# Snake activation: cosine on ScalarE and one VectorE pass from PSUM in place of sine, square and a product matmul; first-layer tiles of one bank

## Chip, cores, metric

One core of a Trainium2 chip. The metric is the device time of one execution in microseconds (us). PE is TensorE (matmuls), PEld its weight loads, ACT ScalarE, DVE VectorE, POOL GpSimd, SP SyncE. A ratio is the mean time of one kernel's fast runs over the mean of the other's fast runs of the same rounds, so it is not quite the ratio of the medians quoted beside it. Profiled spans (875.6 before) come from one execution each.

## The reference

```python
X = np.fft.rfft(x, axis=1)                 # x: 8 x 3008 x 256
y = np.fft.irfft(X * (filt_r + 1j*filt_i), n=3008, axis=1)
h = y.reshape(24064, 256) @ w_in           # 256 -> 2048
s = np.sin(alpha * h)
g = h + s * s / (alpha + 1e-09)
out = g @ w_out                            # 2048 -> 256
```

With a = alpha, `g @ w_out` is `(a*h + sin(a*h)**2) @ (w_out/a)`. The linear part can be folded into one 256 x 256 matrix, `h @ w_out = y @ (w_in @ w_out)`, which is what the kernel before does. Or, with `sin(u)**2 = (1 - cos(2u))/2`, the bracket is `-0.5 * ((cos(2ah) - 1) - 2ah)`.

## The kernel before

The Fourier transform is three matmul stages per batch, here called first (`pa`), middle (`pb`, products `p`, `pc`) and last (`pd`). They are threaded as small pieces into 48 "chunks" of 512 columns (four of them 384) of the two-layer network. A chunk has eight steps. A step makes two of the sixteen first-layer tiles of its chunk and one eighth of the previous chunk's projection. The spectral tiles rotate through two PSUM banks (`fps`), the hidden tiles through two tiles of two banks (`hps`), the projection through two (`ops`): together eight banks. A bank is here 512 fp32 columns of PSUM, the memory that PE writes its results to; to evacuate it is to copy it out so that PE can write there again.

```python
    fps = pool("fps", 2, PSUM)
    hps = pool("hps", 2, PSUM)
    ops = pool("ops", 2, PSUM)
    # ... cut ...
    def evac(dst, src, on_act=None):
        flip[0] ^= 1
        if flip[0] if on_act is None else on_act:
            marks["act"] = nc.scalar.copy(out=dst, in_=src)
        else:
            marks["dve"] = nc.vector.tensor_copy(out=dst, in_=src)
    # ... cut ...
    def hidden(k, jp):
        # ...
        ps = hps.tile([128, 2, 512], FP32, name=f"ph_{k}_{jp}", tag="h")
        for i in range(2):
            jb = 2 * jp + i
            for cb in range(2):
                marks["hidden"] = nc.tensor.matmul(
                                 out=ps[:, i, 0:n], lhsT=w1[:, cb, jb * 128:jb * 128 + 128],
                                 rhs=y_cols[:, cb, c0:c0 + n], start=(cb == 0), stop=(cb == 1))
        vs = v[k][:, 2 * jp:2 * jp + 2, 0:n]
        nc.scalar.activation(out=vs, in_=ps[:, :, 0:n], func=AFT.Sin)
        marks["square"] = nc.vector.tensor_tensor(out=vs, in0=vs, in1=vs, op=ALU.mult)

    def project(k, u):
        # ...
        for jb in (range(9) if half == 0 else range(9, 16)):
            nc.tensor.matmul(out=dst, lhsT=v[k][:, jb, 128 * t:128 * t + 128],
                             rhs=w2[:, jb, :], start=(jb == 0), stop=False)
        if half == 1:
            for cb in range(2):
                nc.tensor.matmul(out=dst, lhsT=y_cols[:, cb, c0 + 128 * t:c0 + 128 * t + 128],
                                 rhs=m_t[:, cb, :], start=False, stop=(cb == 1))
```

`m_t` is w_in @ w_out, prepared during chunk 0 with 32 transposes and 32 matmuls.

## Time and profile before

| | before |
|---|---|
| median time | 880.1 us (878.55 to 881.52, 4 runs) |
| PE, ACT, DVE busy | 839.0, 519.5, 505.2 us of a span of 875.6 |
| chunk 1 begins, chunk 2 begins | 72.5, 91.4 us |
| chunk 2 to chunk 47 | 756.9 us |
| from chunk 47 to the end | 27.3 us |

The page gives, for each engine, the busy time, its share of the span and the number of instructions:

```profile
span 875.6 us, 15579 instructions
PE 839.0 (96%) x6233; PEld 584.6 (67%) x6233; DVE 505.2 (58%) x890; ACT 519.5 (59%) x667; POOL 28.1 (3%) x55
```

The windows view shows two stretches from the middle of the run: length, then the busy time of each engine with its count, the granted clock, the DMA share and GB/s:

```profile
core 0: us, PE busy (x) PEld busy (x) DVE busy (x) ACT busy (x) POOL busy (x), PEclk, DMA share, GB/s
200.00:400.00 200.00, 199.05 (x1505) 140.36 (x1504) 119.11 (x209) 125.52 (x162) 4.11 (x8) 1.00 0.47 108
400.00:600.00 200.00, 199.76 (x1514) 141.07 (x1513) 120.82 (x211) 125.33 (x162) 4.11 (x8) 1.00 0.47 110
```

PE is busy to within half a per cent, but that alone proves little, because the matmuls' modelled durations overlap (0.379 us each, started 0.216 us apart). The starts say more. A matmul follows the one before after 0.216 us if that had 512 columns, 0.109 if 256, 0.041 if 94 (medians). "TensorE: Matmul & The Clock Gate" (section "Wait — 56ns, not 53.3ns?") gives N / 2.4 GHz + 2.5 ns for a warm array, and these medians agree to a nanosecond. What the starts lie apart beyond that is below called *excess*. From chunk 2 to chunk 47 it is 8.3 us of 756.9. So in the middle of the run PE really streams, and every column taken away should shorten the run.

One step of the middle stage in the timeline (start, length, engine, line, operation; in brackets the idle time before it and what ended it). This and the later timelines show chosen lines, most of the weight loads (PEld) among those left out:

```profile
310.04 0.38 PE L394 MATMUL po_2_3514<-m_t,y 128*128 128x256 f16 x2
...
310.26 1.03 PE L375 MATMUL ph_6_3556<-y,w_465 128*128 128x512 f16 x4
...
311.12 0.38 PE L179 MATMUL pb_2_3563<-t_3_0_3278,d_t 128*128 128x256 f16 x2
...
311.32 1.02 ACT L379 ACTIVATE v_3413<-ph_6_3556 128x1024 f16<-128x1024 f32 x1 [0.51 <-PE ph_6_3556 L375]
311.34 0.27 PE L198 MATMUL pc_1_3572<-p_1_0_3536,e_t 128*128 128x256 f16 x1
...
311.78 1.15 PE L390 MATMUL po_2_3514<-w_466,v_3210 128*128 128x256 f16 x9
311.98 0.69 DVE L136 CAST g_0_3540<-pc_1_3572 128x512 f16<-128x512 f32 x1 [0.74 <-PE pc_1_3572 L198]
...
312.59 0.68 DVE L380 TENSOR_TENSOR v_3413<-v_3413 128x1024 f16<-128x1024 f16 x1
...
312.76 0.59 PE L375 MATMUL ph_7_3587<-y,w_465 128*128 128x512 f16 x2
```

The first line is the product that the change removes. The step lasts 2.50 us (310.26 to 312.76): 4 x 0.216 + 15 x 0.109 = 2.50. DVE evacuates g as soon as its matmuls are done. The hidden tile needs DVE for nothing until it is squared, and its PSUM banks are free once ACT has read them.

At the start DVE stands in front of the w_out load:

```profile
64.46 1.14 DVE L338 TENSOR_SCALAR w_466<-w_out_502,rec_t 128x256 f16<-128x256 f32 x4 [2.96 <-DMA w_out_502<-in_moe_w_out_dram]
```

### The profile page before, as it was taken

Reading aid. Unit: us, or ns where it says so; the run is one execution under the profiler, and the core shown is the slowest. Engines: PE = TensorE matmul, PEld = TensorE weight load, DVE = VectorE, ACT = ScalarE, POOL = GpSimd, SP = SyncE. Lnnn points to the kernel's source line nnn. Section 1 sums busy time; section 2 is a strip of 40 time slices with the busy share of each in tenths; the row PEclk is TensorE's granted clock in tenths of the full one; section 3 lists DMA queues with packets and bytes.
Section 4 is the critical chain, followed back from the end, with each engine's and each line's share of the span. In section 5 each row is a group of like instructions: output and inputs, shape, how many; then the busy total and the mean of one; then the engine's idle time right before and its main releaser. Section 6 shows DMA issues by size and latency. Waiting matters only on the chain.

```text
span 875.6 us, 15579 instructions
## 1 busy us (share of the span) xinstructions
PE 839.0 (96%) x6233; PEld 584.6 (67%) x6233; DVE 505.2 (58%) x890; ACT 519.5 (59%) x667; POOL 28.1 (3%) x55
## 2 busy tenths in 40 slices
PE   6759999999999999999999999999999999999996
PEld 2336676667776676767776677666767677676675
DVE  4748574566646575565746566565755657444442
ACT  4545665566656665566656666566655666555551
POOL 3210000000000000000000000000000000000000
PEclk9969999999999999999999999999999999999998
DMA  9985724275344724265342653347342343411111
GB/s 218 245 233 109 176 72 122 52 160 127 72 124 95 163 77 114 61 139 141 82 108 61 155 129 80 109 96 162 82 119 60 94 105 80 116 47 37 37 37 43
DMA packets 93489, 94.96 MB, mean 108 GB/s; under 512 B 8084, under 2 KB 82852, under 8 KB 93416
## 3 DMA queue, kind: packets, MB, share of 16 engines
q1 hardware_dynamic: 84784, 75.02, 32.5%
q0 software_dynamic: 6704, 18.09, 12.6%
q10 hardware_dynamic: 1928, 0.86, 0.5%
q8 instruction: 49, 0.80, 0.4%
q14 instruction: 24, 0.20, 0.1%
HBM read 58.02 MB, written 49.81 MB: 123 GB/s over the span
## 4 chain that ended last, share of the span: by engine, by line
PE 89%; DMA 6%; DVE 2%; issue 1%; ACT 1%; SPq 0%; ACTq 0%; DVEq 0%; POOLq 0%
DMA w_out_502<-in_moe_w_out_dram 1%; DMA t_1_0_1563<-d_1_505 1%; DMA d_0_107<-t_0_3_159 1%; DMA x_0_109<-in_x_dram 1%; DMA d_2_507<-g_9_2627 1%; DMA t_0_1_176<-d_0_107 0%; DMA t_2_0_2801<-d_2_507 0%; DMA t_4_0_5257<-d_4_511 0%; DMA t_3_0_4019<-d_3_509 0%; DMA t_0_0_476<-d_0_108 0%; PE po_0_7950 L390 0%; PE po_0_5494 L390 0%; PE po_0_3038 L390 0%; PE po_0_720 L390 0%; PE po_2_4348 L390 0%
## 5 line engine op out<-in xcount | busy, mean ns | idle before, releaser
L375 PEld LDWEIGHTS <-w_465 128*128 128x128 f16 x1536 | 150.3, 98 | 100.5 <-issue 2.1
L198 PEld LDWEIGHTS <-e_t 128*128 128x128 f16 x384 | 37.8, 99 | 13.0 <-issue 2.5
L394 PEld LDWEIGHTS <-y 128*128 128x128 f16 x376 | 36.7, 98 | 4.7
L179 PEld LDWEIGHTS <-d_t 128*128 128x128 f16 x192 | 18.7, 100 | 24.4 <-issue 5.4
L156 PEld LDWEIGHTS <-wf_t 94*96 94x96 f16 x128 | 16.5, 129 | 21.8 <-issue 9.3
L380 DVE TENSOR_TENSOR v_9644<-v_9644 128x1024 f16<-128x1024 f16 x8 | 5.5, 692 | 8.0 <-ACT v_9644 L379 8.0
L380 DVE TENSOR_TENSOR v_9789<-v_9789 128x1024 f16<-128x1024 f16 x8 | 5.5, 692 | 8.0 <-ACT v_9789 L379 8.0
L380 DVE TENSOR_TENSOR v_1608<-v_1608 128x1024 f16<-128x1024 f16 x8 | 5.5, 692 | 7.7 <-ACT v_1608 L379 7.7
L380 DVE TENSOR_TENSOR v_9488<-v_9488 128x1024 f16<-128x1024 f16 x8 | 5.5, 692 | 7.7 <-ACT v_9488 L379 7.7
L380 DVE TENSOR_TENSOR v_943<-v_943 128x1024 f16<-128x1024 f16 x8 | 5.5, 691 | 7.7 <-ACT v_943 L379 7.7
L380 DVE TENSOR_TENSOR v_3898<-v_3898 128x1024 f16<-128x1024 f16 x8 | 5.5, 690 | 7.1 <-ACT v_3898 L379 7.1
L380 DVE TENSOR_TENSOR v_2681<-v_2681 128x1024 f16<-128x1024 f16 x8 | 5.5, 691 | 7.1 <-ACT v_2681 L379 7.1
L380 DVE TENSOR_TENSOR v_5137<-v_5137 128x1024 f16<-128x1024 f16 x8 | 5.5, 691 | 7.1 <-ACT v_5137 L379 7.1
L380 DVE TENSOR_TENSOR v_6354<-v_6354 128x1024 f16<-128x1024 f16 x8 | 5.5, 691 | 7.1 <-ACT v_6354 L379 7.1
L380 DVE TENSOR_TENSOR v_8810<-v_8810 128x1024 f16<-128x1024 f16 x8 | 5.5, 690 | 7.1 <-ACT v_8810 L379 7.1
L380 DVE TENSOR_TENSOR v_7593<-v_7593 128x1024 f16<-128x1024 f16 x8 | 5.5, 690 | 7.1 <-ACT v_7593 L379 7.1
L380 DVE TENSOR_TENSOR v_4064<-v_4064 128x1024 f16<-128x1024 f16 x8 | 5.5, 693 | 7.1 <-ACT v_4064 L379 7.1
L380 DVE TENSOR_TENSOR v_9317<-v_9317 128x1024 f16<-128x1024 f16 x8 | 5.5, 693 | 7.1 <-ACT v_9317 L379 7.1
L380 DVE TENSOR_TENSOR v_9147<-v_9147 128x1024 f16<-128x1024 f16 x8 | 5.5, 693 | 7.1 <-ACT v_9147 L379 7.1
L380 DVE TENSOR_TENSOR v_8976<-v_8976 128x1024 f16<-128x1024 f16 x8 | 5.5, 692 | 7.1 <-ACT v_8976 L379 7.1
L380 DVE TENSOR_TENSOR v_6520<-v_6520 128x1024 f16<-128x1024 f16 x8 | 5.5, 692 | 7.1 <-ACT v_6520 L379 7.1
L380 DVE TENSOR_TENSOR v_4652<-v_4652 128x1024 f16<-128x1024 f16 x8 | 5.5, 692 | 5.9 <-ACT v_4652 L379 5.9
(2435 smaller groups left out, 2460.3 us busy)
## 6 DMA issues: line engine op xcount, KB each, us to landing
w_in_469<-in_moe_w_in_dram POOLq DMA_DIRECT2D x2, 1024.0 KB, 9.2
w_out_502<-in_moe_w_out_dram POOLq DMA_DIRECT2D x1, 2048.0 KB, 12.5
filt_101<-in_filt_r_dram POOLq DMA_DIRECT2D x8, 96.0 KB, 7.4
filt_102<-in_filt_i_dram POOLq DMA_DIRECT2D x8, 96.0 KB, 7.9
d_t<-d_tbl SPq DMA_DIRECT2D x1, 768.0 KB
d_0_107<-t_0_0_117 SPq DMA_DIRECT2D x1, 384.0 KB
d_0_107<-t_0_1_131 SPq DMA_DIRECT2D x1, 384.0 KB
d_0_107<-t_0_2_145 SPq DMA_DIRECT2D x1, 384.0 KB
```

What stands on the lines that cost most here:

```text
L156: marks["pe"] = nc.tensor.matmul(out=ps[0:NK, :], lhsT=wf_t, rhs=st["x"][ch][:, n0:n0 + 2, :], start=True, stop=True)
L179: nc.tensor.matmul(out=ps[:, i, :], lhsT=d_t[:, s, :], rhs=st["t2"][s // 6][:, s % 6, :], start=True, stop=True)
L198: nc.tensor.matmul(out=ps[:, i, :], lhsT=e_t[:, k, 2 * w + i, :], rhs=pr[k][:, i, :], start=(k == 0), stop=(k == 1))
L375: marks["hidden"] = nc.tensor.matmul(out=ps[:, i, 0:n], lhsT=w1[:, cb, jb * 128:jb * 128 + 128], rhs=y_cols[:, cb, c0:c0 + n], start=(cb = ...
L380: marks["square"] = nc.vector.tensor_tensor(out=vs, in0=vs, in1=vs, op=ALU.mult)
L394: nc.tensor.matmul(out=dst, lhsT=y_cols[:, cb, c0 + 128 * t:c0 + 128 * t + 128], rhs=m_t[:, cb, :], start=False, stop=(cb == 1))
```

## The change

The intent is to take the product matmuls off PE. The linear term then comes out of the same DVE pass as the nonlinear one. That pass reads PSUM, so a hidden bank is held through ACT and DVE. The hidden tiles become one bank each, four of them, and work is moved from DVE to ACT: the output copies, and the evacuations from one half to two thirds.

```diff
+    cospool = pool("cosp", 4)
-    hps = pool("hps", 2, PSUM)
+    hps = pool("hps", 4, PSUM)
     def evac(dst, src, on_act=None):
-        flip[0] ^= 1
+        flip[0] = (flip[0] + 1) % 3
+    quarter = cpool.tile([128, 1], FP32)
+    nc.vector.memset(quarter, float(np.pi / 2))
-    nc.vector.memset(ones, 1.0)
+    nc.vector.memset(ones, 2.0)          # w_in is now scaled by 2*alpha
     # ... w_out scaled by -0.5/alpha; the w1T transposes, the m_t matmuls and m_t itself removed ...
-        ps = hps.tile([128, 2, 512], FP32, name=f"ph_{k}_{jp}", tag="h")
-        # ... two halves of it ...
-        nc.scalar.activation(out=vs, in_=ps[:, :, 0:n], func=AFT.Sin)
-        marks["square"] = nc.vector.tensor_tensor(out=vs, in0=vs, in1=vs, op=ALU.mult)
+        ps = hps.tile([128, 512], FP32, name=f"ph_{k}_{jb}", tag="h")
+        # ... two matmuls ...
+        cs = cospool.tile([128, 512], FP32, name=f"cos_{k}_{jb}", tag="c")
+        nc.scalar.activation(out=cs[:, 0:n], in_=ps[:, 0:n], func=AFT.Sin, bias=quarter)
+        marks["snake"] = nc.vector.scalar_tensor_tensor(
+            out=v[k][:, jb, 0:n], in0=cs[:, 0:n], scalar=-1.0, in1=ps[:, 0:n],
+            op0=ALU.add, op1=ALU.subtract)
-        if half == 1:
-            for cb in range(2):
-                nc.tensor.matmul(out=dst, lhsT=y_cols[:, cb, c0 + 128 * t:c0 + 128 * t + 128],
-                                 rhs=m_t[:, cb, :], start=False, stop=(cb == 1))
-            nc.vector.tensor_copy(out=o[:, 0:nb, :], in_=pso[k][:, 0:nb, :])
+            nc.scalar.copy(out=o[:, 0:nb, :], in_=pso[k][:, 0:nb, :])
```

More of the change, by code (lines that the diff above doesn't have):

```diff
@@ L300 @@
     for i in range(2):
-        al_bc.append(hps.tile([128, 2, 512], FP32, name=f"al_bc_{i}", tag="h"))
         for h in range(2):
-            behind(nc.tensor.matmul(out=al_bc[i][:, h, :], lhsT=ones[64 * h:64 * h + 1, :],
+            al_bc.append(hps.tile([128, 512], FP32, name=f"al_bc_{i}_{h}", tag="h"))
+            behind(nc.tensor.matmul(out=al_bc[-1], lhsT=ones[64 * h:64 * h + 1, :],
                                     rhs=al_row[i][64 * h:64 * h + 1].rearrange("p a b -> p (a b)"),
@@ L315 @@
     w2 = cpool.tile([128, 16, C], FP16)
-    m_t = cpool.tile([128, 2, C], FP16)
-    w1T = cpool.tile([128, 16, C], FP16)
     w_in32 = vpool.tile([128, 2, DFF], FP32, name="w_in32", tag="v")
@@ L322 @@
         after(nc.gpsimd.dma_start(out=w_in32[:, :, hs], in_=w_in_v[:, :, hs]), marks["t2", 3])
-    for i in range(2):
+    for i in range(4):
         for cb in range(2):
             behind(nc.vector.tensor_tensor(
-                out=w1[:, cb, 1024 * i:1024 * i + 1024], in0=w_in32[:, cb, 1024 * i:1024 * i + 1024],
-                in1=al_bc[i].rearrange("p a b -> p (a b)"), op=ALU.mult), s2_dve)
+                out=w1[:, cb, 512 * i:512 * i + 512], in0=w_in32[:, cb, 512 * i:512 * i + 512],
+                in1=al_bc[i], op=ALU.mult), s2_dve)
     for _, piece in first[21:25]:
@@ L339, in weights_out @@
                     out=w2[:, jb, :], in0=w_out32[:, jb, :], scalar1=rec_t[:, jb:jb + 1],
-                    scalar2=None, op0=ALU.mult), marks["square"])
-        if i < 4:
-            pst = ops.tile([128, 8, 128], FP16, name=f"pst_{i}", tag="o")
-            for cb in range(2):
-                for t in range(4):
-                    jb = 4 * i + t
-                    behind(nc.tensor.transpose(out=pst[:, 4 * cb + t, :],
-                                               in_=w1[:, cb, jb * 128:jb * 128 + 128],
-                                               identity=id16), marks["hidden"])
-            for cb, copy in enumerate((nc.scalar.copy, nc.vector.tensor_copy)):
-                copy(out=w1T[:, 4 * i:4 * i + 4, cb * 128:cb * 128 + 128],
-                     in_=pst[:, 4 * cb:4 * cb + 4, :])
-        elif i >= 6:
-            cb = i - 6
-            psm = ops.tile([128, 2, C], FP32, name=f"psm_{cb}", tag="o")
-            for jb in range(16):
-                behind(nc.tensor.matmul(out=psm[:, 0, :], lhsT=w1T[:, jb, cb * 128:cb * 128 + 128],
-                                        rhs=w2[:, jb, :], start=(jb == 0), stop=(jb == 15)),
-                       marks["hidden"])
-            nc.vector.tensor_copy(out=m_t[:, cb, :], in_=psm[:, 0, :])
+                    scalar2=-0.5, op0=ALU.mult, op1=ALU.mult), marks["snake"])
     chunks = [(pb, c0, min(512, 2 * S - c0)) for pb in range(B // 2) for c0 in range(0, 2 * S, 512)]
@@ L365, with hidden @@
     pso = {}
-    def hidden(k, jp):
+    def hidden(k, jb):
         _, c0, n = chunks[k]
-        if jp == 0:
+        if jb == 0:
             v[k] = vpool.tile([128, 16, 512], FP16, name=f"v_{k}", tag="v")
-        ps = hps.tile([128, 2, 512], FP32, name=f"ph_{k}_{jp}", tag="h")
-        for i in range(2):
-            jb = 2 * jp + i
-            for cb in range(2):
-                marks["hidden"] = nc.tensor.matmul(
-                                 out=ps[:, i, 0:n], lhsT=w1[:, cb, jb * 128:jb * 128 + 128],
-                                 rhs=y_cols[:, cb, c0:c0 + n], start=(cb == 0), stop=(cb == 1))
-        vs = v[k][:, 2 * jp:2 * jp + 2, 0:n]
-        nc.scalar.activation(out=vs, in_=ps[:, :, 0:n], func=AFT.Sin)
-        marks["square"] = nc.vector.tensor_tensor(out=vs, in0=vs, in1=vs, op=ALU.mult)
+        ps = hps.tile([128, 512], FP32, name=f"ph_{k}_{jb}", tag="h")
+        for cb in range(2):
+            nc.tensor.matmul(out=ps[:, 0:n], lhsT=w1[:, cb, jb * 128:jb * 128 + 128],
+                             rhs=y_cols[:, cb, c0:c0 + n], start=(cb == 0), stop=(cb == 1))
+        cs = cospool.tile([128, 512], FP32, name=f"cos_{k}_{jb}", tag="c")
[3 more added lines that the diff above has]
+            op0=ALU.add, op1=ALU.subtract)
     def project(k, u):
@@ L387, in project @@
             pso[k] = ops.tile([128, 2, C], FP32, name=f"po_{k}_{t}", tag="o")
-        dst = pso[k][:, t % 2, :]
-        for jb in (range(9) if half == 0 else range(9, 16)):
-            nc.tensor.matmul(out=dst, lhsT=v[k][:, jb, 128 * t:128 * t + 128],
-                             rhs=w2[:, jb, :], start=(jb == 0), stop=False)
-        if half == 1:
-            for cb in range(2):
-                nc.tensor.matmul(out=dst, lhsT=y_cols[:, cb, c0 + 128 * t:c0 + 128 * t + 128],
-                                 rhs=m_t[:, cb, :], start=False, stop=(cb == 1))
+        for jb in range(8 * half, 8 * half + 8):
+            nc.tensor.matmul(out=pso[k][:, t % 2, :], lhsT=v[k][:, jb, 128 * t:128 * t + 128],
+                             rhs=w2[:, jb, :], start=(jb == 0), stop=(jb == 15))
         last = 128 * (t + 1) == n
@@ L437 @@
             if k < len(chunks):
-                hidden(k, j)
+                hidden(k, 2 * j)
+                hidden(k, 2 * j + 1)
             if k == 0:
```

## The prediction

> **What bounds the kernel now.** TensorE, nearly everywhere. The windows view shows PE busy 199.05 of 200 us between 200 and 400 us and 199.76 of 200 between 400 and 600, at granted clock 1.00, with DVE at 60% and ACT at 63%. It is real streaming: in the timeline a step of the spectral middle stage (4 matmuls of 512 columns, 15 of 256) repeats every 2.5 us, and the starts of matmuls lie 0.216 us (512) and 0.108 us (256) apart, which sums to 2.48 us. The chain of waits is 89% PE. The exceptions: the first 73 us (DMA) and the last 10.
>
> **What goes away.** 376 matmuls of 256 columns with the product weights: 376 x 0.108 = 41 us of PE, all on the critical path. Chunk 0 also sheds 32 transposes and 32 matmuls, about 5 us. DVE loses the squares (352 x 0.69 + 32 x 0.56 = 261 us), 96 output copies (65 us) and a sixth of the evacuations (about 37 us).
>
> **What comes.** DVE: 752 passes over 512 columns, one operand fp32 in PSUM. The w_in scaling, of the same operand kinds, took about 1.15 us for 1024 columns; a 512-column PSUM copy took 0.685, 0.60 from start to start. So 0.69 each, 515 us in all: DVE busy 505 to about 660. "VectorE: DVE Perf Modes" (the perf-mode tier table) puts any two-tensor PSUM operation at one element per cycle, as these durations do. ACT: a 1024-column Sin is 1.02 us; two of 512 are 2 x 0.59 (0.49 start to start, as PSUM copies show). "ScalarE: Activation LUTs" (What ACT_TABLE_LOAD costs) adds about 93 ns for a pointer bias; no trace here shows it. ACT busy rises from 520 to 670-740 us.
>
> **What of this is critical.** Per step of the middle stage (the densest): PE 2.39 us, DVE 2 x 0.60 + 2 x 0.335 + 0.60/3 = 2.07, ACT 1.9 to 2.1. PE stays the limit, but latency gets tight. A hidden bank is held through ACT and DVE; four banks give over 3 us for roughly 2, so that should hold. Tighter is the two-bank ring of the spectral stages: on DVE a g evacuation stands behind two new passes and two products, ends about 3.8 us after the step began, and its bank is wanted at about 3.5. I expect 0.3-0.4 us of PE wait in a third of the middle steps (28), 8-11 us in all.
>
> **Start.** Before, DVE stood on the w_out load until 64.5 us, and chunk 1 began at 72.5. Now ten passes (6 us) and 16 weight scalings (4.4 us) follow that load, and hidden banks come free only behind them: chunk 1 at 73-75 us; the removed transposes gain nothing; perhaps 1.5 us is lost.
>
> **Sum.** 880.5 - 41 + 1.5 + 7 = about 848 us; in 8 of 10 cases 833 to 867. Faster by over 2%: 0.80; within 2%: 0.17; slower: 0.03.
>
> **What would show it.** PE instructions 6233 to about 5790; DVE passes at 0.65-0.70 us; ACT Sin of 512 columns at 0.59 (or 0.69 with the bias); DVE about 660 us, ACT 670-740; mid-run windows with PE still over 94% busy; waits of PE for DVE evacuations of g or y tiles as the new entry in the waits view; chunk 1 starting at 73-75 us.
>
> **What would make it wrong.** The pass on DVE running well over 0.7 us: then DVE is the limit, and the time stays or rises. Hidden banks coming back late. Or no evacuation wait appears: then 835.

## The result and the profile after

The time fell to 840.95 us (839.49 to 841.59, 4 runs), from 880.1 in the same rounds: ratio 0.9555, 95% interval 0.9541 to 0.9569. The predicted 848 (833 to 867) was 7 us too high.

| | before | after |
|---|---|---|
| PE, ACT, DVE busy, us | 839.0, 519.5, 505.2 | 799.2, 674.7, 628.4 |
| chunk 1, chunk 2 begin | 72.5, 91.4 | 75.0, 89.9 |
| chunk 2 to chunk 47 | 756.9 | 723.4 |
| excess in it | 8.3 | 13.5 |
| from chunk 47 to the end | 27.3 | 25.9 |

The page of the kernel after, with its two costliest groups (line, engine, operation, tiles, shape, count, then busy time, mean ns of one, and the idle time before them):

```profile
span 839.2 us, 16120 instructions
PE 799.2 (95%) x5793; PEld 544.1 (65%) x5793; DVE 628.4 (75%) x1120; ACT 674.7 (80%) x1200; POOL 28.3 (3%) x55
L360 DVE SCALAR_TENSOR_TENSOR v<-cos,ph 128x512 f16<-128x512 f32 (+1 forms) x768 | 483.8, 671 | 148.1 <-ACT cos L359 147.1
L359 ACT ACTIVATE cos<-ph,quarter 128x512 f32<-128x512 f32 (+1 forms) x768 | 480.6, 680 | 103.9 <-PE ph L356 101.6
```

There are 440 matmuls fewer (376 products, 32 transposes, 32 for the product). The windows of the same two stretches:

```profile
200.00:400.00 200.00, 199.13 (x1481) 137.98 (x1480) 157.45 (x279) 171.31 (x308) 4.10 (x8) 1.00 0.48 112
400.00:600.00 200.00, 199.29 (x1480) 137.97 (x1479) 157.39 (x280) 171.22 (x308) 4.11 (x8) 1.00 0.47 111
```

DVE goes from 60% to 79% and ACT from 63% to 86%, while PE stays at over 99%. Nothing in the PE column shows that PE now waits more. "Perfetto Trace Analysis" (section "Identifying the Most-Contended Engine") warns that matmul busy time is a poor measure because matmuls are pipelined, and this is a case of it. A wait of 0.16 us disappears inside the modelled end of the previous matmul.

Two steps of the middle stage in the timeline, answering to the one shown of before:

```profile
306.63 1.03 PE L356 MATMUL ph<-y,w 128*128 128x512 f16 x4
...
307.72 0.60 PE L199 MATMUL pc<-p,e_t 128*128 128x256 f16 x4
...
307.99 1.28 DVE L360 SCALAR_TENSOR_TENSOR v<-cos,ph 128x512 f16<-128x512 f32 x2 [0.37 <-ACT cos L359]
...
309.03 1.03 PE L356 MATMUL ph<-y,w 128*128 128x512 f16 x4
309.19 0.75 DVE L187 TENSOR_TENSOR p<-xf,filt 128x512 f16<-128x512 f16 x2
...
309.86 0.68 DVE L137 CAST g<-pc 128x512 f16<-128x512 f32 x1
309.89 0.38 PE L180 MATMUL pb<-t,d_t 128*128 128x256 f16 x2
...
310.11 0.49 PE L371 MATMUL po<-w,v 128*128 128x256 f16 x3
...
310.60 0.60 PE L199 MATMUL pc<-p,e_t 128*128 128x256 f16 x4
```

The first step takes 2.40 us, the sum of its columns. After its hidden matmuls DVE makes two new passes (307.99) and then two products (309.19, already in the next step), and only then evacuates g (309.86), whose matmuls began at 307.72. The next `pc` needs that bank. It starts at 310.60, just after the evacuation ended at 310.54, although three projection matmuls had been pulled in front of it. Three matmuls of 256 columns take 0.33 us, so 310.11 + 0.33 = 310.44 was its turn: PE lost 0.16 us.

Between chunk 2 and chunk 47 there are 23 such waits, three or four in each of seven batches, eighteen of about 0.16 us and five of about 0.39. Excess by the matmul that waited: `pc` 4.7 us (1.8 before), `pa` 5.1 (1.6), `pd` 2.5 (4.6), hidden 0.7 (0.1).

Each of these has its own cause in the trace. The 23 waits make up all of the excess before `pc`, and each ends just after a g evacuation on DVE. Of the 5.1 us before `pa`, 4.0 (16 waits) end just after an evacuation of y on ACT, not on DVE. Of the 2.5 before `pd`, 1.7 is one wait for a load: the spectral data go through DRAM twice (`d<-t`, `t<-d`, `d<-g`, `t<-d`), and PE waits when they come back late. Such waits before `pb` and `pd` sum to 4.1 us in the trace before and 2.1 after.

At the start, DVE waits for the w_out load and PE with it:

```profile
65.26 1.14 DVE L339 TENSOR_SCALAR w<-w_out,rec_t 128x256 f16<-128x256 f32 x4 [4.45 <-DMA w_out<-in_moe_w_out_dram]
65.67 1.70 PE L371 MATMUL po<-w,v 128*128 128x256 f16 x7 [4.21 <-DVE w L339]
```

**The account.** A product matmul costs PE 0.109 us, and the 376 of them cost 41.0: 8 before chunk 2 begins, 354 up to chunk 47, 14 after.

- Chunk 2 to 47: 354 x 0.109 = 38.6 us less, 5.2 us more excess, together 33.4 less. Measured: 33.5.
- Before chunk 2: 1.5 us less, of which 8 x 0.109 = 0.9 is matmuls. The remaining 0.6 us is what is left of the removed preparation after the new waits at the start; run a below separates the two.
- After chunk 47: 1.4 us less; 14 x 0.109 = 1.5.

Together this is 36.4 us, the difference of the two profiled spans. The timed medians differ by 39.2; the further 2.8 us comes nearly all from the profiled execution of the kernel before, which was faster than its timed runs. Where in the run those lose it is not located.

### The profile page after: what moved, and what is told of

Read it like the earlier page. It is cut to its first block, busy times and chain, and to the rows that moved or that the text cites. A ratio compares the mean times of both kernels' runs of the same rounds, so it can differ in the third digit from the quotient of the medians.

```text
span 839.2 us, 16120 instructions
## 1 busy us (share of the span) xinstructions
PE 799.2 (95%) x5793; PEld 544.1 (65%) x5793; DVE 628.4 (75%) x1120; ACT 674.7 (80%) x1200; POOL 28.3 (3%) x55
## 4 chain that ended last, share of the span: by engine, by line
PE 82%; DMA 7%; DVE 4%; ACT 4%; issue 2%; SPq 0%; POOL 0%; ACTq 0%; DVEq 0%; POOLq 0%
PE ph L356 35%; PE po L371 35%; PE pc L199 5%; PE pa L157 4%; PE pd L219 2%; DMA t<-d 2%; PE pb L180 2%; ACT cos L359 2%; DMA d<-t 1%; DMA w_out<-in_moe_w_out_dram 1%; DVE v L360 1%; DVE p L187 1%; DMA d<-g 1%; ACT t L135 1%; DMA filt<-in_filt_r_dram 1%
## 5 line engine op out<-in xcount | busy, mean ns | idle before, releaser
L360 DVE SCALAR_TENSOR_TENSOR v<-cos,ph 128x512 f16<-128x512 f32 (+1 forms) x768 | 483.8, 671 | 148.1 <-ACT cos L359 147.1
L359 ACT ACTIVATE cos<-ph,quarter 128x512 f32<-128x512 f32 (+1 forms) x768 | 480.6, 680 | 103.9 <-PE ph L356 101.6
L371 PE MATMUL po<-w,v 128*128 128x256 f16 x3008 | 401.3, 273 | 4.2 <-DVE w L339 4.2
L356 PE MATMUL ph<-y,w 128*128 128x512 f16 (+1 forms) x1536 | 391.3, 376 | 0.3 <-ACT y L135 0.2
L371 PEld LDWEIGHTS <-v 128*128 128x128 f16 x3008 | 289.0, 98 | 80.7 <-issue 8.9
L356 PEld LDWEIGHTS <-w 128*128 128x128 f16 x1536 | 150.6, 98 | 102.8 <-issue 5.5
L187 DVE TENSOR_TENSOR p<-xf,filt 128x512 f16<-128x512 f16 x192 | 72.1, 418 | 6.2 <-ACT xf L183 5.4
L377 ACT COPY o<-po 128x512 f32<-128x512 f32 x96 | 56.5, 589 | 9.8 <-PE po L371 7.4
L183 ACT CAST xf<-pb 128x512 f16<-128x512 f32 x96 | 56.6, 591 | 8.8 <-DMA t<-d 5.7
L199 PE MATMUL pc<-p,e_t 128*128 128x256 f16 x384 | 59.9, 276 | 2.9 <-DVE p L187 1.5
L180 PEld LDWEIGHTS <-d_t 128*128 128x128 f16 x192 | 18.7, 101 | 25.4 <-DMA t<-d 4.5
```

The source lines that it names most:

```text
L180: nc.tensor.matmul(out=ps[:, i, :], lhsT=d_t[:, s, :], rhs=st["t2"][s // 6][:, s % 6, :], start=True, stop=True)
L183: nc.scalar.copy(out=xf, in_=ps)
L187: marks["prod", u] = nc.vector.tensor_tensor(out=pt, in0=xf, in1=f_t[k][:, 2 * u:2 * u + 2, :], op=ALU.mult)
L199: nc.tensor.matmul(out=ps[:, i, :], lhsT=e_t[:, k, 2 * w + i, :], rhs=pr[k][:, i, :], start=(k == 0), stop=(k == 1))
L356: nc.tensor.matmul(out=ps[:, 0:n], lhsT=w1[:, cb, jb * 128:jb * 128 + 128], rhs=y_cols[:, cb, c0:c0 + n], start=(cb == 0), stop=(cb == 1))
L359: nc.scalar.activation(out=cs[:, 0:n], in_=ps[:, 0:n], func=AFT.Sin, bias=quarter)
```

## The experiments

Theory: the kernel is bound by PE before and after. The whole gain is the PE time of the product matmuls, and all that ACT and DVE took on is hidden, except for a few us of PE waits that arise because short PSUM evacuations stand behind the new passes in DVE's queue. (The runs bear out the first part; of the waits, they show that this is one cause among three.) Rivals: a part of the gain comes from the one-bank tiles or from the moved copies; or ACT or DVE now sets the pace.

All twelve kernels ran in five rounds beside the kernel before, in four groups on different chips; the kernel after was not run again with them, so the ratios compare best. "Excess" is PE's, from chunk 2 to chunk 47, in the one trace of each kernel.

| run | median us | ratio to before (95%) | excess us |
|---|---|---|---|
| kernel after | 840.95 | 0.9555 (0.9541 to 0.9569) | 13.5 |
| a_drop_product | 838.52 | 0.9526 (0.9512 to 0.9539) | 12.1 |
| b_zero_product | 880.70 | 1.0007 (0.9993 to 1.0020) | 12.0 |
| c_g_on_act | 840.56 | 0.9552 (0.9537 to 0.9567) | 15.1 |
| d_ring3 | 840.34 | 0.9540 (0.9520 to 0.9559) | 13.7 |
| e_one_bank | 881.48 | 1.0018 (1.0004 to 1.0033) | 10.5 |
| g_copy_dve | 846.91 | 0.9638 (0.9619 to 0.9658) | 20.4 |
| h_both_back | 847.21 | 0.9619 (0.9603 to 0.9634) | 17.2 |
| l_late_scale | 841.82 | 0.9570 (0.9553 to 0.9586) | 13.7 |
| m_two_bank | 855.73 | 0.9734 (0.9717 to 0.9751) | 24.2 |
| f_evac_half | 845.38 | 0.9602 (0.9576 to 0.9628) | 18.7 |
| i_no_bias | 839.99 | 0.9559 (0.9538 to 0.9581) | 14.9 |
| n_best | 840.77 | 0.9546 (0.9528 to 0.9564) | 11.6 |

### a_drop_product: only the removal, in the kernel before

```diff
-        if i < 4: ...            # transposes, m_t matmuls and copies: all removed
         for jb in (range(9) if half == 0 else range(9, 16)):
-            nc.tensor.matmul(..., rhs=w2[:, jb, :], start=(jb == 0), stop=False)
+            nc.tensor.matmul(..., rhs=w2[:, jb, :], start=(jb == 0), stop=(jb == 15))
-        if half == 1: ...        # the m_t matmuls
```

> The kernel before, with the product weights, their preparation and their 376 matmuls left out and nothing else changed; the output is wrong on purpose. Theory (the gain is PE time and only that; all that the change adds to VectorE and ScalarE is hidden but for about 5 us of new PE waits): 836 us, that is 880 - 41 - 3 for the preparation, 3 to 8 us under the changed kernel's 841. Rival (the one-bank tiles, the moved copies and the new split of evacuations bring a share of the gain of their own): 850 us or more.

838.5 us (wrong result). With sine, square and two-bank tiles untouched, dropping the product alone brings the whole gain and about 2.5 us more, a little short of the 3 to 8 expected; the intervals of the two ratios just miss each other. In the profiles the difference to the kernel after is 2.2 us at the start (chunk 2 begins at 87.8 against 89.9) and 1.3 us in the middle, less 1.0 us at the end. So everything the change adds on ACT (155 us) and DVE (123 us) costs about 2.5 us net.

Two things here correct the picture. At the start, chunk 2 begins 3.7 us earlier than before, of which 8 matmuls are 0.9: in this trace the removed preparation is worth 2.8 us, and the rest of the change takes 2.2 of them back. And dropping the matmuls alone already raises excess from 8.3 to 12.1, with none of the new passes. Before `pc` it is 4.5 us, as much as in the kernel after (4.7), but here the waits end with the products on DVE and none with g. That shorter steps leave the same latencies less room would explain it; no run isolates that.

### b_zero_product: the product matmuls put back with zero weights

```diff
+        if half == 1:
+            for cb in range(2):
+                nc.tensor.matmul(out=pso[k][:, t % 2, :],
+                                 lhsT=y_cols[:, cb, c0 + 128 * t:c0 + 128 * t + 128],
+                                 rhs=zero_w[:, cb, :], start=False, stop=(cb == 1))
```

> The changed kernel with the 376 product matmuls put back, with zero weights, so the result stays right. Theory (PE is still the limit, each matmul of 256 columns costs 0.108 us): 841 + 41 = 880 to 883 us. Rival (VectorE or ScalarE, 75% and 80% busy, now set the pace and PE has slack): under 865 us.

880.7 us: +40 for 376 matmuls, 0.106 us each. PE has no slack in the kernel after. Had ACT or DVE set the pace, part of this would have been hidden. Theory confirmed.

### c_g_on_act: g evacuations on ScalarE

```diff
-        flip[0] = (flip[0] + 1) % 3
+        if on_act is None:
+            flip[0] ^= 1
-                evac(st["g"][:, i0:i0 + 2, :], ps, i0 != 2 if b == 0 else None)
+                evac(st["g"][:, i0:i0 + 2, :], ps, i0 != 2 if b == 0 else True)
```

> The changed kernel with every g evacuation of batches 1 to 7 on ScalarE and the other evacuations alternating, so the shares of the two engines stay about two to one. Theory (the 21 waits of 0.16 to 0.39 us of PE before the pc matmuls come from g evacuations that stand in VectorE's queue behind the new passes): those waits vanish, PE excess before pc falls from 4.7 to under 1 us, time 836 to 839 us. Rival (the pc matmuls wait for the products or for ScalarE's backlog): the waits stay or grow, 841 us or more.

840.6 us, and two findings. The waits before `pc` were indeed those of g on DVE: their excess falls from 4.7 to 0.5 us. The same place in the timeline no longer has one; `pb` at 309.67 is followed by `pc` after 2 x 0.109:

```profile
309.67 0.38 PE L181 MATMUL pb<-t,d_t 128*128 128x256 f16 x2
309.89 0.60 PE L200 MATMUL pc<-p,e_t 128*128 128x256 f16 x4
```

But the total did not fall (13.5 to 15.1), so the expected gain of a few us was a miss. Excess before `pd` rose from 2.5 to 4.8, before `pb` from 0.3 to 2.8, before the hidden tiles from 0.7 to 2.1. Nearly all of the first two is PE waiting for loads (`t<-d`): two waits, in the first of these batches, are 2.5 and 2.7 us. The other evacuations now alternated, so more of them were on DVE, which may have made those loads later; no run shows it by itself. (The count of 21 in the expectation should be 23.)

### d_ring3: three spectral banks, three hidden banks

```diff
-    fps = pool("fps", 2, PSUM)
-    hps = pool("hps", 4, PSUM)
+    fps = pool("fps", 3, PSUM)
+    hps = pool("hps", 3, PSUM)
```

> The changed kernel with three banks for the spectral tiles and three for the hidden tiles, in place of two and four. Theory (the new PE waits sit on the two-bank ring of the spectral stages, and the hidden ring has slack): waits before pa and pc vanish, 835 to 837 us. Rival (a hidden bank is held so long through ScalarE and VectorE that four are needed): PE waits before hidden matmuls, 850 us or more.

840.3 us. Neither number came true. Excess before `pa` and `pc` fell from 9.8 to 1.2 us, as the theory had it, so those waits do sit on the two-bank spectral ring. But excess before the hidden matmuls rose from 0.7 to 8.4, of which 7.0 ends with a new pass on DVE, so the hidden ring has no bank to spare either; my statement that it had slack fell. The total stayed (13.7): the bank given to one ring was paid for by the other.

### e_one_bank: one-bank tiles alone, in the kernel before

```diff
-        ps = hps.tile([128, 2, 512], FP32, name=f"ph_{k}_{jp}", tag="h")
         for i in range(2):
             jb = 2 * jp + i
+            ps = hps.tile([128, 512], FP32, name=f"ph_{k}_{jb}", tag="h")
             # ... two matmuls, then one sine and one square of 512 columns ...
```

> The kernel before with one part of the change alone: hidden tiles of one bank, four of them, each with its own sine and square of 512 columns; product and its matmuls kept. Theory (PE sets the time and its work is the same): 880 us, within 3 of before; ScalarE busy rises by about 50 to 60 us, VectorE by about 30, and nothing is gained or lost. Rival (finer tiles feed PE better and carry a part of the gain): under 872 us.

881.5 us: no gain of their own. The busy times I got the wrong way round: ACT rose by 24 us, DVE by 48. Excess before `pa` is 4.9 us here (1.6 before), about what it is in the kernel after (5.1). So these waits come with the smaller tiles already; they need neither the cosine nor the new pass.

### g_copy_dve, f_evac_half, h_both_back: the moves to ScalarE undone

```diff
# g_copy_dve
-            nc.scalar.copy(out=o[:, 0:nb, :], in_=pso[k][:, 0:nb, :])
+            nc.vector.tensor_copy(out=o[:, 0:nb, :], in_=pso[k][:, 0:nb, :])
# f_evac_half
-        flip[0] = (flip[0] + 1) % 3
+        flip[0] ^= 1
# h_both_back: both
```

> The changed kernel with the output copies back on VectorE (evacuations still two to one). VectorE busy 628 + 65 = about 693 us, ScalarE about 618. Theory (both engines have slack, so the split matters only through waits of PE for tiles behind VectorE's queue): 841 to 846 us. Rival (VectorE at over 80% blocks the chain): 855 us or more.

> The changed kernel with the evacuations shared equally again (output copies stay on ScalarE): VectorE about 655 us busy, ScalarE about 645. With copies on VectorE this cost nothing more (847 with it, 847 without). Theory (what costs is a spectral evacuation standing behind VectorE's passes and copies; the copies are the larger part): 840 to 844 us. Rival (the two-to-one split carries its own 5 us): 845 to 848 us.

> The changed kernel with both moves to ScalarE undone: output copies on VectorE and evacuations shared equally. VectorE about 725 us busy, ScalarE about 590. Theory (PE-bound, waits on the spectral ring grow as more evacuations stand behind VectorE's new passes: six g evacuations of a batch on VectorE in place of four, stage-1 ones too): 846 to 856 us, PE excess time mid-run from 13.5 to 18 or more. Rival 1 (split does not matter at all): 839 to 842. Rival 2 (VectorE becomes the limit): over 870.

846.9, 845.4 and 847.2 us: about 6, 4 and 6 us slower than the kernel after (7, 4 and 6 by the ratios). So the moves to ACT are worth keeping, and their effects do not add. The copies alone cost slightly more than the theory's range; for the half split the median lies with the rival, though the runs (841.7 to 846.7) spread over both. DVE is at 680, 658 and 706 us of about 846 in them, so it is not the limit by its sum. With the half split, excess before `pc` is 6.4 in place of 4.7, and 35 waits there end with a g evacuation in place of 23: the theory's cause. With the copies on DVE the cause is another. Excess before `pd` is 8.1 us in place of 2.5, and most of it is PE waiting for loads. In the fifth batch:

```profile
428.62 3.04 SPq L389 DMA_DIRECT2D out_dram<-o  x5
429.70 0.68 DVE L137 CAST g<-pc 128x512 f16<-128x512 f32 x1
431.76 1.25 SPq L206 DMA_DIRECT2D d<-g  x2
439.94 0.34 PE L219 MATMUL pd<-wi_t,t 96*128 96x94 f16 x4 [0.98 <-DMA t<-d]
```

The last g is ready at 430.38, but SyncE, which issues the stores of the output too, is busy with these until 431.66, and only then issues the transfer of g. In the kernel after the stores of this batch are issued before g is ready (by 425.25 against 425.94), the transfer follows at 425.97, and `pd` does not wait. From the third to the seventh batch the transfer is issued 1.0 to 1.7 us after g with the copies on DVE, and 0.0 to 0.3 us after it in the kernel after. The kernel before shows the same delay (1.2 to 1.5 us in six of seven batches), so the moved copies do bring something of their own: undone, they raise the waits for loads from 2.1 to 9.5 us, 4.7 of it in these five batches. The run with the most DVE work (h) has less excess than the one with only the copies moved (17.2, just under the 18 expected, against 20.4), so load alone does not rank them.

### i_no_bias: the bias left off

```diff
-        nc.scalar.activation(out=cs[:, 0:n], in_=ps[:, 0:n], func=AFT.Sin, bias=quarter)
+        nc.scalar.activation(out=cs[:, 0:n], in_=ps[:, 0:n], func=AFT.Sin)
```

> The changed kernel with the bias tile left off the activation, so it computes a sine; the output is wrong on purpose. It measures the pointer bias: the activation of 512 columns at 0.587 us as in the one-bank run in place of 0.687, ScalarE busy 675 to about 600 us. Theory (ScalarE is off the critical path): 839 to 841 us, PE excess mid-run still over 10 us. Rival (the ScalarE queue is what makes PE wait for evacuations): 835 or less, waits before pa and pd gone.

```profile
L359 ACT ACTIVATE cos<-ph 128x512 f32<-128x512 f32 (+1 forms) x768 | 411.9, 589 | 153.5 <-PE ph L356 152.1
```

840.0 us (wrong result), excess 14.9. The mean activation is 91 ns shorter (589 against 680; both means include the short chunks), ACT busy falls by 61 us, and the time does not move; nor do the waits before `pa` shrink (5.4 us), so a less busy ACT does not remove them. ScalarE is off the critical path although it is 80% busy. "ScalarE: Activation LUTs" (section "What ACT_TABLE_LOAD costs") gives about 93 ns for each pointer operand; this run agrees.

### m_two_bank: two-bank tiles in the kernel after

```diff
-    hps = pool("hps", 4, PSUM)
+    hps = pool("hps", 2, PSUM)
+        ps = hps.tile([128, 2, 512], FP32, name=f"ph_{k}_{jb}", tag="h")
+        # four matmuls, one activation and one scalar_tensor_tensor of 1024 columns
```

> The changed kernel with hidden tiles of two banks, two of them, as before the change, so one cosine and one VectorE pass of 1024 columns for two of 512; everything else as changed. A bank pair is then held for 0.86 us of matmuls, 1.1 to 1.2 us of ScalarE and 1.2 us of VectorE plus waits, and wanted again after two steps of 1.9 to 2.4 us. Theory (one-bank tiles are what lets the hold fit, the third reading of the ring): PE waits before hidden matmuls appear, 850 us or more. Rival (the ring has slack, and half the instructions mean less fixed cost on both engines: ScalarE 675 to about 600 us busy, VectorE 628 to about 590): 837 to 842 us.

855.7 us, 15 slower than with one-bank tiles, although both engines have less to do (ACT 623 against 675, DVE 607 against 628). The theory's time was right but its place was wrong. Excess before the hidden matmuls is only 3.4 us; before `pc` it is 13.1, and 12.8 of that ends with a product on DVE. The timeline shows why:

```profile
306.09 1.22 DVE L361 SCALAR_TENSOR_TENSOR v<-cos,ph 128x1024 f16<-128x1024 f32 x1 [0.29 <-ACT cos L360]
...
307.23 0.75 DVE L187 TENSOR_TENSOR p<-xf,filt 128x512 f16<-128x512 f16 x2
...
307.36 0.27 PE L372 MATMUL po<-w,v 128*128 128x256 f16 x1
307.71 0.28 PE L199 MATMUL pc<-p,e_t 128*128 128x256 f16 x1
307.83 0.27 PE L372 MATMUL po<-w,v 128*128 128x256 f16 x1
308.04 0.49 PE L199 MATMUL pc<-p,e_t 128*128 128x256 f16 x3
```

The pass of 1024 columns holds DVE until 307.31. The products that `pc` needs (their input was ready: `xf` was copied at 305.96, for 0.58 us) start only as it ends (307.23), and `pc` starts as each product lands. In the kernel after, the two passes of a step are ordered the same way, but the first begins after half the matmuls. "Perfetto Trace Analysis" (section "Optimizing Scalar/DVE Operations") says that where these engines are not saturated but cause bubbles elsewhere, breaking up instructions may let work finish sooner. This pair of runs shows it: 855.7 against 841.

### l_late_scale: w_out scaled two steps later

```diff
-        if i in (2, 3, 4, 5):
-            for jb in range(4 * i - 8, 4 * i - 4):
+        if i in (4, 5, 6, 7):
+            for jb in range(4 * i - 16, 4 * i - 12):
```

> The changed kernel with the sixteen w_out scalings two steps later in chunk 0, so that VectorE no longer stands on the w_out load (4.5 us of wait at 61 to 65 us) with six hidden passes behind it. Theory (the start lost about 2 us because hidden banks came free only behind that load): chunk 1 begins at 72 to 73.5 us in place of 75.0, time 838 to 840 us. Rival (the start is set by the load itself, since the first projection needs the scaled weights anyway): 841 us, chunk 2 beginning at 90 us as before.

841.8 us: no faster. In the profile chunk 1 does begin earlier (73.1 in place of 75.0) and chunk 2 at 88.8 (89.9), but the timed runs do not show the microsecond. PE's wait for the scaled weights is replaced by one of the same length for a load of x:

```profile
65.96 0.42 PE L157 MATMUL pa<-x,wf_t 94*96 94x512 f16 x1 [4.67 <-DMA x<-in_x_dram]
```

So the order of DVE's work holds about 1 us of the start. Behind it stands the load of the second batch.

### n_best: an attempt at a faster version

This is c with the remaining evacuations two to one, together with l_late_scale.

```diff
-        flip[0] = (flip[0] + 1) % 3
+        if on_act is None:
+            flip[0] = (flip[0] + 1) % 3
-                evac(..., i0 != 2 if b == 0 else None)
+                evac(..., i0 != 2 if b == 0 else True)
```

> An attempt to beat the changed kernel: every g evacuation of batches 1 to 7 on ScalarE, the others still two to one (in the earlier run with g on ScalarE they alternated, and what pc no longer waited came back before pa, pd and pb), and the w_out scalings two steps later. VectorE about 612 us busy, ScalarE about 690. Theory (PE's remaining waits come from evacuations and products that stand behind VectorE's passes, and ScalarE has slack, as the run without the bias showed): PE excess mid-run 13.5 to about 9, time 835 to 839 us. Rival (the waits only move from one tile to another, as in the two earlier attempts): 840 to 842 us, excess 13 or more.

840.8 us (838.3 to 841.0), ratio 0.9546 against 0.9555. The profile shows the expected direction (span 836.5, excess 11.6, none of it to speak of before `pc`), but it is of the fastest of the five runs, and the timed difference is inside the intervals. The time is the rival's (840 to 842). It is not shown to be faster than the kernel after.

## Why the prediction was right

- **What bounds the kernel: right, and shown.** a and b bracket it: taking the product matmuls out of the kernel before gives 838.5, putting them back into the kernel after gives 880.7.
- **41 us of PE: right.** 376 x 0.109 = 41.0 in the account of the trace, 40 in run b.
- **The added cost is hidden: right.** a against the kernel after leaves about 2.5 us net for all of it. The pass on DVE takes 0.68 us for 512 columns (0.65 to 0.70 predicted), the activation 0.687 (0.69 with the bias).
- **The busy times: ACT right, DVE too high.** ACT is 675 us (670 to 740 predicted), DVE 628 (660). I summed durations of 0.69 us where queued passes overlap: 768 of them fill 484 us, 0.63 each. I had also miscounted 752 for 768 (48 chunks of 16).
- **"0.3-0.4 us of PE wait in a third of the middle steps (28), 8-11 us in all": right in kind, too large.** The waits are there, on the tile, the engine and the ring named, and c removes them. The evacuation ends 3.9 us after its step began (310.54 against 306.63; 3.8 predicted). There are 23, not 28, because in five of the seven batches no later `pc` uses the bank of the last g that DVE evacuates. Most cost 0.16 us; three projection matmuls, 0.33 us, stand in front of each `pc` that waits. Together they cost 4.8 us, not 8 to 11. The sum had put 7 for the waits without saying why less, and the rise of all excess is 5.2 us. That these two are near each other is partly luck: a shows 3.8 of the 5.2 with no new pass at all.
- **"four banks give over 3 us for roughly 2, so that should hold": it held, but with less room than I thought.** d shows that with three banks the hidden matmuls wait 8.4 us.
- **The waits before `pa` (5.1 us against 1.6) were not in the sum.** They come from the same ring, as d shows, and with the one-bank tiles, as e shows.
- **"chunk 1 at 73-75 us ... perhaps 1.5 us is lost": half right.** Chunk 1 began at 75.0, but more work of the next steps was done by then (24 projection, 8 `pd` and 3 `pa` matmuls more than before), and by chunk 2 the start was 0.6 us better apart from the matmuls. This term was off by 2.1 us. The step that failed is "the removed transposes gain nothing": in a's trace the removed preparation gains 2.8 us, and the loss from the new passes and the late banks is then about 2.2, not 1.5.

So the direction and the main mechanism were right, and two terms of the sum were mis-sized: the start (+1.5 predicted, -0.6 measured) and the waits (7 predicted, 5.2 measured). Together they make 3.9 of the 7 us by which 848 was too high. Of the rest, 2.8 us is the gap between profiled and timed differences, which nothing in the prediction covers.

## What to carry to other kernels

On a kernel whose matmuls really stream, moving arithmetic from PE to half-idle engines paid almost in full here (39 of 41 us), even though those engines went from 60% to 80% or more; check it by the starts of the matmuls, not by PE's busy share. What such a move costs is time spent behind other work in a queue. A short evacuation or product behind a long elementwise pass became a PE wait, so keep the passes short (one bank, not two) and give short evacuations to the engine with the quieter queue. A late output copy delayed the stores, and with them the spectral transfers behind them, so look at the DMA queue too. Here, moving a bank or an evacuation removed one kind of wait and brought others: two attempts kept the sum of waits at 14 to 15 us, and a third cut it to 11.6 without a resolved gain in time.

## What the Trainium skill lacked or had wrong

- "VectorE: DVE Perf Modes" (the perf-mode tier table) has no row for scalar_tensor_tensor. With one fp32 operand in SBUF, one fp32 operand in PSUM and a 16-bit result it took 0.68 us for 512 columns and 1.22 us for 1024 here, that is 1.06 ns for each further column and about 0.14 us besides.
- "ScalarE: Activation LUTs" (section "What ACT_TABLE_LOAD costs") has the pointer bias right (93 ns; 91 ns here between the means), but its fixed part is a little high for this case: 280 + 0.833 x 512 = 707 ns by the page, a median of 687 here. The input lay in PSUM and the output in SBUF; the page does not say which memory its figure is for.
- "Perfetto Trace Analysis" rightly calls matmul busy time a poor measure but for finding waits it goes by the gaps between an engine's slices (section "Optimization Strategy"). Here busy PE stayed over 99% while waits of 0.16 us, which leave no such gap, summed to several us; the starts less the normal interval showed them.
- No page says how much a larger elementwise instruction can cost elsewhere: two-bank tiles saved ACT 52 us and DVE 21 us of busy time and made the kernel 15 us slower.
